# P times V on eight 64x32 array tiles instead of four 128x32 ones

## The chip, the cores and the metric

The kernel runs on one core of a Trainium2 chip. The metric is device time in microseconds of one execution. The core has five engines that matter here, each with an instruction queue of its own that is worked off in order: PE (TensorE, matmuls into PSUM), DVE (VectorE), ACT (ScalarE), POOL (GpSimd, which here works on SBUF only) and SP (SyncE, here the issuer of DMAs). PSUM has eight banks, each 128 partitions by 512 float32.

## The reference

One transformer block with attention and a gated MLP side by side, on x of 2048 tokens by 640:

```python
xn = _layernorm(x)
qkv = (xn @ wqkv)...            # 32 heads, 20 wide
scores = einsum("bhqd,bhkd->bhqk", q, k) * 20 ** -0.5
mask = (i - j >= 0) & (i - j < 256)      # a query sees itself and the 255 keys before it
o = einsum("bhqk,bhkd->bhqd", softmax(where(mask, scores, -1e9)), v)
h = gelu(xn @ w_gate) * (xn @ w_up)
out = x + o @ wo + h @ w_down
```

Everything is float32. The change is in the second `einsum`, the product of the softmax weights P with V.

## The kernel before

The work has three stages. The first (to about 60 us) normalises x, transposes it and begins the projections. The second (about 60 to 571 us) is attention, with the projections and part of the MLP woven between as filling for PE. The third is the rest of the MLP and the output product.

Attention goes in 32 units. Unit u is a group of four heads (g = u // 4) and a chunk of 512 queries (c = u % 4). For a unit the kernel does this:

- `max_pair` (lines 502 to 538): scores once in bfloat16 on 64x64 array tiles, into `ps_m` banks. DVE takes their row maximum (line 526). Eight pairs of banks in a unit.
- `exp_piece` (line 567): the scores again, transposed (keys on the partitions), into a bank `ps_e` (line 581), and ACT writes their exponentials into an SBUF tile `P` (line 583). `pieces(c)` (line 548) packs the key blocks of 128 that a chunk sees into three P tiles called X, Z and Y in `pieces`, of four heads each. For c > 0 there are six key blocks, b-2 to b+3 with b = 4c. X holds b and b-2, Z holds b-1 and b+2, Y holds b+1 and b+3. For c = 0 there are four blocks, 0 to 3. The twelve steps s = 0 to 11 of a unit are X, Z, Y with four heads each.
- `clear` (line 587): after the fourth head of a P tile, POOL zeroes the corners of the band that the mask excludes, one `affine_select` (line 594 or 597) for each 128x128 corner, all four heads at once. Y has three of them, the last for block b+3.
- `av_unit` (line 600): the product. For each key block and each of the four heads one float32 matmul: 128 keys by 32 columns of V (20 of V, one column of ones that gives the softmax sum, the rest unused) as stationary operand, P as the moving one. Head j writes PSUM partitions 32j to 32j+31 of one bank `ps_o`, so four 128x32 tiles of the array work side by side. ACT copies the bank to the SBUF tile `ob` (line 612), and SP stores it (lines 616 and 617).

All of `ps_m`, `ps_e`, `ps_n` and `ps_o` are taken from one pool of six PSUM banks (`bank`, line 497). The first matmul into a bank waits for the engine that read the bank's former content.

What sets the order is written out by hand in `attention` (line 804): a unit has 14 slots. In slot 0 the loop issues two `max_pair`, the product of the unit before, two more `max_pair`, and step s = 0 of its own scores. Steps 1 to 4 are in slot 2, 5 and 6 in slot 4, 7 and 8 in slot 8, and 9 to 11 in slot 10. `defer(n, ...)` puts work n slots later. `clear` of a P tile comes one slot after its last step, so Y is cleared in slot 11, three slots ahead of the product. Each slot ends with some 2.4 dense matmuls of filling. POOL also makes low parts of split weights (line 642, in steps of 128x128), low parts of q and k (line 259) and sums of x (line 739).

A float32 matmul shows as two records of one length in the profile, each with its own weight load. The product therefore has 704 matmuls in the program and 1408 records at line 608: 48 records in a unit with c > 0, 32 in a unit with c = 0.

Of the kernel before, what the change touches and what calls it, by code (L numbers as in the profile page):

```python
# [9 lines left out]
F32 = mybir.dt.float32  # L10
F32R = mybir.dt.float32r
BF = mybir.dt.bfloat16
AF = mybir.ActivationFunctionType
OP = mybir.AluOpType
# [5 lines left out]
C = 512  # L20
# [50 lines left out]
def block_kernel(ctx, tc, x, wqk, wv, wgu, wdo, wdl, out):  # L71
    nc = tc.nc
# [120 lines left out]
    done = set()  # L193
    now = [None]

    def at(slot, fn, *a):
        acts.setdefault(slot, []).append((fn, a))
# [31 lines left out]
    def defer(n, fn, *a):  # L229
        if now[0] is None:  # L230
            fn(*a)
        else:
            at(now[0] + n, fn, *a)
# [190 lines left out]
    with tc.tile_pool(name="lp", bufs=1, side="right") as lp:  # L424
# [5 lines left out]
        ps = psd.tile([128, C], F32, name="ps_u", tag="dn")  # L430
# [48 lines left out]
    vtiles = dict(enumerate(v0[2]))  # L479
    pf.close()  # L480
    psr = pp.enter_context(tc.tile_pool(name="psr", bufs=6, space=PSUM, reuse_waits="tile"))
    ap = pr.enter_context(tc.tile_pool(name="ap", bufs=2, side="right", reuse_waits="tile"))
# [14 lines left out]
    def bank(name):  # L497
        return psr.tile([128, C], F32, name=name, tag="ring")
# [49 lines left out]
    def pieces(c):  # L548
        b = 4 * c
        X = [(b, 0, 0, 384)] + ([(b - 2, 384, 0, 128)] if c else [])  # L550
        Y = [(b + 1, 0, 128, 384), (b + 3, 384, 384, 128)]
        Z = ([(b - 1, 0, 0, 256)] if c else []) + [(b + 2, 256, 256, 256)]
        return X, Z, Y
# [11 lines left out]
    pts = {}  # L565
# [21 lines left out]
    def clear(u, bi):  # L587
        c = u % NC
        pt = pts[u, bi]
        for p in pieces(c)[bi]:  # L590
            for col, diag in diag_tail(*p, c):
# [4 lines left out]
                else:  # L596
                    nc.gpsimd.affine_select(out=a, in_=a, pattern=[[0, 4], [-1, 128]], compare_op=OP.is_ge,  # L597
                                            fill=0.0, base=-1, channel_multiplier=1)

    def av_unit(u):  # L600
        g, c = divmod(u, NC)
        o, v = bank("ps_o"), vtiles[g]
        todo = [(pts[u, bi], *p) for bi, ps in enumerate(pieces(c)) for p in ps]
        for i, (pt, kb, col, q0, n) in enumerate(todo):
            assert (id(v), kb) in done, (u, kb)
            for j in range(4):
                w0_ = kb * 84 + 21 * j
                nc.tensor.matmul(o[32 * j:32 * j + 32, q0:q0 + n], v[:, w0_:w0_ + 32], pt[:, j, col:col + n],  # L608
                                 start=i == 0, stop=i == len(todo) - 1, skip_group_check=True,
                                 tile_position=(0, 32 * j))  # L610
        ob = ap.tile([128, C], F32, name="ob", tag="ob", bufs=1)
        nc.scalar.activation(ob, o, AF.Copy)  # L612

        def store():
            for j in range(4):
                nc.sync.dma_start(od[c].rearrange("(d h) t -> h d t", h=H)[4 * g + j], ob[32 * j:32 * j + DH, :])
            nc.sync.dma_start(sd[c][4 * g:4 * g + 4, :], ob[DH::32, :])

        defer(3, store)

    def load_gu(f):
        raws = []
# [715 lines left out]
    for j, f in enumerate(range(NFA, NF - 1)):  # L1338
        end = f + 1 == NF - 1
        first, second = {i: [] for i in range(4)}, {i: [] for i in range(4)}  # L1340
# [91 lines left out]
    for n, (p, k) in enumerate(steps):  # L1432
        i = n % (NQD + 1)
        if i == 0:
            begun.clear()
            ps = {b: psn.tile([128, C], F32, name=f"ps_{b}", tag=f"b{b}") for b in (1, 2, 5, 3, 6, 4, 7, 8)}
# [71 lines left out]
```

## Time and profile before

| | |
|---|---|
| median of 3 runs | 1047.59 us (1047.58 to 1047.95) |
| the profiled execution, span from first to last instruction | 1046.8 us |
| PE busy | 1035.2 us (99%), 7997 matmul records |
| weight loads (PEld) busy | 827.6 us (79%) |
| DVE busy | 730.8 us (70%) |
| ACT busy | 513.5 us (49%) |
| POOL busy | 333.8 us (32%), in attention 274 of 464 us |
| granted PE clock | 0.999 of full |
| product P times V, line 608 | 84.3 us of PE |
| copies of `ps_o`, line 612 | 19.1 us of ACT, 32 of 597 ns |

The span is what the trace covers. The run times are 0.8 us longer, for what lies ahead of the first and behind the last instruction. Busy time of PE is the union of its records, and a record of a matmul includes its way through the array, so neighbours overlap. Starts of successive rows tell what PE spends, the durations don't. In rows of a timeline the first number is the start, the second the length of the whole merged row, `x48` the number of records in it, and a bracket says how long the engine was idle before and what ended that.

### The profile page before, as it was taken

The numbers are of one execution on the slowest core, as the hardware profiler recorded it, in microseconds if no ns is written. First come the engines' busy times: TensorE is split into PE (matmuls) and PEld (weight loads), VectorE is DVE, ScalarE is ACT, GpSimd is POOL, SyncE is SP. The second block draws the span as 40 slices with busy tenths as digits, with TensorE's granted clock in tenths as the row PEclk, the third lists the DMA queues.
The fourth block names the chain that finished last, engine by engine and source line by source line (L and its number), as shares of the span: only waits on it lengthen the run. The fifth ranks groups of instructions, "written<-read, shape, count | busy, mean of one in ns | idle before, by whom it ended". The sixth has DMA issues, their size and how long they took to land.

```text
span 1046.8 us, 22733 instructions
## 1 busy us (share of the span) xinstructions
PE 1035.2 (99%) x7997; PEld 827.6 (79%) x7997; DVE 730.8 (70%) x2007; ACT 513.5 (49%) x1088; POOL 333.8 (32%) x503
## 2 busy tenths in 40 slices
PE   8999999999999999999999999999999999999998
PEld 7987666666677766666666888888888999999998
DVE  8745656666665556677662677877655889888887
ACT  4444666765665566656565532223324554333332
POOL 5122667766464458474635111110110000000000
PEclk9999999999999999999999999999999999999999
DMA  5651465545332344444322557677217874443342
GB/s 200 189 150 59 135 183 159 179 148 180 96 117 72 111 145 144 139 130 130 112 79 75 191 189 244 213 251 253 100 61 250 270 241 137 134 128 113 125 134 94
DMA packets 105179, 158.56 MB, mean 151 GB/s; under 512 B 15420, under 2 KB 60092, under 8 KB 105064
## 3 DMA queue, kind: packets, MB, share of 16 engines
q1 hardware_dynamic: 102680, 150.95, 45.0%
q10 hardware_dynamic: 2384, 6.16, 1.9%
q8 instruction: 63, 1.03, 0.4%
q14 instruction: 52, 0.43, 0.1%
HBM read 101.78 MB, written 54.92 MB: 150 GB/s over the span
## 4 chain that ended last, share of the span: by engine, by line
PE 92%; DVE 3%; DMA 2%; ACT 1%; POOL 1%; issue 1%; SPq 0%; DVEq 0%; POOLq 0%; ACTq 0%
PE ps_g L952 21%; PE ps L1219 21%; PE ps_d L110 21%; PE ps_e L581 8%; PE ps_o L608 7%; PE ps_v L110 7%; PE ps_m L522 4%; PE ps_g L110 1%; PE ps_t L181 1%; DVE junk L526 1%; DMA qs<-qd 1%; PE ps_d L356 1%; DVE ss L1057 0%; POOL pt L259 0%; DVE at L1057 0%
## 5 line engine op out<-in xcount | busy, mean ns | idle before, releaser
L526 DVE CUSTOM_DVE_ANT_0 junk<-ps_m,mask 128x320 bf16<-128x320 f32 (+2 forms) x512 | 243.2, 475 | 144.5 <-PE ps_m L522 85.5
L583 ACT ACTIVATE P<-ps_e 128x512 f32<-128x512 f32 (+2 forms) x384 | 195.6, 578 | 60.9 <-PE ps_e L581 59.0
L1219 PE MATMUL ps<-wb,at 128*128 128x320 f32 x999 | 156.0, 309 | 0.0
L1219 PEld LDWEIGHTS ps<-wb,at 128*128 128x128 f32 x999 | 148.9, 188 | 0.3
L594 POOL TENSOR_SCALAR_AFFINE_SELECT P<-P 128x512 f32<-128x512 f32 x128 | 83.9, 657 | 141.0 <-ACT P L583 138.3
L581 PE MATMUL ps_e<-qs,ks 124*128 124x128 bf16 (+2 forms) x704 | 108.0, 277 | 0.7 <-DVE mx L526 0.4
L110 PE MATMUL ps_d<-xh,wqh 128*128 128x512 f32 x350 | 104.4, 410 | 0.0
L110 PE MATMUL ps_d<-xl,wqh 128*128 128x512 f32 x350 | 104.2, 409 | 0.0
L110 PE MATMUL ps_d<-xh,wql 128*128 128x512 f32 x350 | 103.8, 409 | 0.0
L1219 PE MATMUL ps<-wt,at 128*128 128x320 f32 x552 | 89.2, 309 | 0.4 <-DVE u L1057 0.4
L581 PEld LDWEIGHTS <-ks 124*128 124x128 bf16 x704 | 50.8, 98 | 47.8 <-issue 30.1
L608 PE MATMUL ps_o<-P,v 128*32 128x384 f32 (+2 forms) x1408 | 84.3, 386 | 0.6 <-DVE mx L526 0.6
L1219 PEld LDWEIGHTS ps<-wt,at 128*128 128x128 f32 x552 | 82.9, 188 | 0.9 <-DVE u L1057 0.9
L597 POOL TENSOR_SCALAR_AFFINE_SELECT P<-P 128x512 f32<-128x512 f32 x112 | 70.8, 643 | 33.7 <-ACT P L583 33.7
L1173 ACT ACTIVATE at<-ss 128x512 fp32r<-128x512 f32 x59 | 37.3, 632 | 89.6 <-DVE ss L1057 89.6
L103 POOL TENSOR_TENSOR wql<-wr,wqh 128x640 fp32r<-128x640 f32 x11 | 17.6, 1607 | 174.0 <-PE ps_g L952 129.4
L110 PEld LDWEIGHTS ps_d<-xh,wql 128*128 128x128 f32 x350 | 63.9, 189 | 11.1 <-issue 0.3
L608 PEld LDWEIGHTS ps_o<-P,v 128*32 128x32 f32 x1408 | 41.5, 110 | 39.0 <-issue 21.1
L110 PEld LDWEIGHTS ps_d<-xl,wqh 128*128 128x128 f32 x350 | 63.8, 189 | 10.5 <-issue 0.2
L110 PEld LDWEIGHTS ps_d<-xh,wqh 128*128 128x128 f32 x350 | 63.4, 189 | 10.7 <-issue 0.3
L259 POOL TENSOR_TENSOR pt<-r,pt 128x512 bf16<-128x512 f32 x40 | 46.8, 1170 | 67.3 <-ACT pt L258 67.2
L612 ACT ACTIVATE ob<-ps_o 128x512 f32<-128x512 f32 x32 | 19.1, 597 | 86.6 <-PE ps_o L608 72.3
(194 smaller groups left out, 1846.0 us busy)
## 6 DMA issues: line engine op xcount, KB each, us to landing
hr<-hd SPq DMA_DIRECT2D x104, 128.0 KB
hd<-he SPq DMA_DIRECT2D x50, 256.0 KB
wr<-wgu SPq DMA_DIRECT2D x27, 320.0 KB
qs<-qd SPq DMA_DIRECT2D x64, 120.0 KB
ks<-kd SPq DMA_DIRECT2D x64, 120.0 KB
xi<-x SPq DMA_DIRECT2D x16, 320.0 KB
qs<-qd SPq DMA_DIRECT2D x64, 80.0 KB
ks<-kd SPq DMA_DIRECT2D x64, 80.0 KB
```

The costliest lines, as they stand in the source:

```text
L110: nc.tensor.matmul(ps, a(k), b(k), start=n == 0, stop=n == 3 * nk - 1)
L259: nc.gpsimd.tensor_tensor(out=pt[:, l, :], in0=r, in1=pt[:, 1, :], op=OP.subtract)
L522: nc.tensor.matmul(ps[64 * h:64 * h + 64, lo:hi], q[rows, j, q0:q0 + 64], keys, start=True, stop=True, tile_position=(64 * r, 64 * h))
L526: nc.vector.tensor_tensor_reduce(out=junk[:, 0:n], in0=ps[:, 0:n], in1=mask[:, 320 - n:320], scale=1.0, scalar=NEG, op0=OP.add, op1=OP.max ...
L581: nc.tensor.matmul(ps[:, col:col + n], k[0:QROWS, j, kc:kc + 128], q[0:QROWS, j, q0:q0 + n], start=True, stop=True)
L583: nc.scalar.activation(pt[:, j, lo:hi], ps[:, lo:hi], AF.Exp, scale=SCALE)
L594: nc.gpsimd.affine_select(out=a, in_=a, pattern=[[0, 4], [1, 128]], compare_op=OP.is_ge, fill=0.0, base=0, channel_multiplier=-1)
L597: nc.gpsimd.affine_select(out=a, in_=a, pattern=[[0, 4], [-1, 128]], compare_op=OP.is_ge, fill=0.0, base=-1, channel_multiplier=1)
L608: nc.tensor.matmul(o[32 * j:32 * j + 32, q0:q0 + n], v[:, w0_:w0_ + 32], pt[:, j, col:col + n], start=i == 0, stop=i == len(todo) - 1, ski ...
L952: nc.tensor.matmul(ps, i, j, start=first and n == 0, stop=n == len(work) - 1, skip_group_check=True)
L1173: nc.scalar.activation(hi[:, 3:7], s, AF.Copy)
L1219: nc.tensor.matmul(ps[bank][:, 0:HD], *work[bank][j], start=bank not in begun, stop=final[p, bank] == n and j == len(work[bank]) - 1, skip ...
```

## The change

The key block of 128 is cut into two halves of 64 keys. Each half is a 64x32 tile of the array (rows 0 to 63 or 64 to 127, columns of head j), so eight tiles work where four did. The halves write two banks. A half of 64 keys is seen by 319 queries at most, so its matmul is up to 320 columns wide where that of the block was up to 384. `windows` gives each half its columns and pairs a lower half with an upper half of the same width (for c = 0 with that of the same block). The six pairs of a unit with c > 0 are 320, 128, 64, 256, 192 and 320 columns wide, 1280 in all where the six blocks had 1536. With c = 0 the four pairs are 320/384, 320/320, 256/192 and 128/64, 1024 and 960 where the blocks had 1152.

ACT copies the first bank to `ob` as before, and the second one into the part of the Y tile of P that belongs to head 0, which the product has read by then. One slot later POOL adds the two, and the store comes one slot later than it did.

```diff
+    def windows(c):
+        r = {}
+        for bi, ps in enumerate(pieces(c)):
+            for kb, col, q0, n in ps:
+                for h in range(2):
+                    first = 128 * (kb - 4 * c) + 64 * h
+                    lo = max(0, first) if kb else 0
+                    hi = min(C, first + 320)
+                    r[h, kb - 4 * c] = bi, kb, col + lo - q0, lo, hi - lo
+        pairs = [((0, 0), (1, 0)), ((0, 3), (1, -2)), ((0, -2), (1, 3)), ((0, 2), (1, -1)), ((0, -1), (1, 2)),
+                 ((0, 1), (1, 1))]
+        if not c:
+            pairs = [((0, d), (1, d)) for d in range(4)]
+        return [[(h, *r[h, d]) for h, d in p] for p in pairs]
+
     def av_unit(u):
         g, c = divmod(u, NC)
-        o, v = bank("ps_o"), vtiles[g]
-        todo = [(pts[u, bi], *p) for bi, ps in enumerate(pieces(c)) for p in ps]
-        for i, (pt, kb, col, q0, n) in enumerate(todo):
-            assert (id(v), kb) in done, (u, kb)
+        halves, v = [bank("ps_o") for _ in range(2)], vtiles[g]
+        todo = windows(c)
+        for i, pair in enumerate(todo):
             for j in range(4):
-                w0_ = kb * 84 + 21 * j
-                nc.tensor.matmul(o[32 * j:32 * j + 32, q0:q0 + n], v[:, w0_:w0_ + 32], pt[:, j, col:col + n],
-                                 start=i == 0, stop=i == len(todo) - 1, skip_group_check=True,
-                                 tile_position=(0, 32 * j))
-        ob = ap.tile([128, C], F32, name="ob", tag="ob", bufs=1)
-        nc.scalar.activation(ob, o, AF.Copy)
+                for h, bi, kb, col, q0, n in pair:
+                    assert (id(v), kb) in done, (u, kb)
+                    rows, w0_ = slice(64 * h, 64 * h + 64), kb * 84 + 21 * j
+                    nc.tensor.matmul(halves[h][32 * j:32 * j + 32, q0:q0 + n], v[rows, w0_:w0_ + 32],
+                                     pts[u, bi][rows, j, col:col + n], start=i == 0, stop=i == len(todo) - 1,
+                                     skip_group_check=True, tile_position=(64 * h, 32 * j))
+        ob, other = ap.tile([128, C], F32, name="ob", tag="ob", bufs=1), pts[u, 2][:, 0, :]
+        nc.scalar.activation(ob, halves[0], AF.Copy)
+        nc.scalar.activation(other, halves[1], AF.Copy)
+        defer(1, lambda: nc.gpsimd.tensor_tensor(out=ob, in0=ob, in1=other, op=OP.add))
...
-        defer(3, store)
+        defer(4, store)
```

Line numbers behind the edit are 18 higher. The order of the instructions moves at three places, shown here for unit 13 (c = 1). A row is a line, an operation, output and inputs and the output's shape; a bracket names the engines or DMA queues that it waits for.

On PE, the product before. It begins with the two blocks of X, goes on with Z, and has Y last. It waits for POOL at each block's first matmul where that block has a cleared corner:

```order
L608 MATMUL ps_o<-P,v 32x384 [waits Activation_49,Pool_49]
L608 MATMUL ps_o<-P,v 32x384 x3
L608 MATMUL ps_o<-P,v 32x128 [waits Pool_49]
L608 MATMUL ps_o<-P,v 32x128 x3
L608 MATMUL ps_o<-P,v 32x256 [waits Pool_49]
L608 MATMUL ps_o<-P,v 32x256 x3
L608 MATMUL ps_o<-P,v 32x256 [waits Pool_49]
L608 MATMUL ps_o<-P,v 32x256 x3
L608 MATMUL ps_o<-P,v 32x384 [waits Pool_49]
L608 MATMUL ps_o<-P,v 32x384 x2
L608 MATMUL ps_o<-P,v 32x384 [waits Activation_49]
L608 MATMUL ps_o<-P,v 32x128 [waits Pool_49]
```

The product now:

```order
L624 MATMUL ps_o<-P,v 32x320 [waits Activation_49,Pool_49]
L624 MATMUL ps_o<-P,v 32x320 [waits Activation_49]
L624 MATMUL ps_o<-P,v 32x320 x6
L624 MATMUL ps_o<-P,v 32x128 [waits Pool_49]
L624 MATMUL ps_o<-P,v 32x128 x7
L624 MATMUL ps_o<-P,v 32x64 x8
L624 MATMUL ps_o<-P,v 32x256 x8
L624 MATMUL ps_o<-P,v 32x192 x8
L624 MATMUL ps_o<-P,v 32x320 x8
```

The second pair is the lower half of block b+3 beside the upper half of b-2. The wait for POOL at its first matmul is for the last corner of Y, which was the last wait of the product before and is now the second one.

On PE, directly behind the product's four `max_pair` banks, the first score of the next unit (s = 0). Before:

```order
L522 LDWEIGHTS qs_166
L522 MATMUL ps_m<-ks_172,qs_166 64x320
L581 LDWEIGHTS ks_170 [waits DMAHW2_49,DMAHW0_49]
L581 MATMUL ps_e<-qs_168,ks_170 128x128 [waits DVE_49]
L581 LDWEIGHTS ks_171
L581 MATMUL ps_e<-qs_168,ks_171 128x384
```

And now:

```order
L522 LDWEIGHTS qs_166
L522 MATMUL ps_m<-ks_172,qs_166 64x320
L581 LDWEIGHTS ks_170 [waits DMAHW2_49,DMAHW0_49]
L581 MATMUL ps_e<-qs_168,ks_170 128x128 [waits Activation_49]
L581 LDWEIGHTS ks_171
L581 MATMUL ps_e<-qs_168,ks_171 128x384
```

With one bank more in use, this score takes the bank of the product's first half. Its wait was for a DVE maximum and is now for ACT's copy of that half (line 628). It is so in the 30 units that have a unit with scores behind them.

On POOL, from the clears of Z to those of the next X. Before:

```order
L597 AFFINE_SELECT P<-P 128x4x128 [waits Activation_49]
L594 AFFINE_SELECT P<-P 128x4x128
L594 AFFINE_SELECT P<-P 128x4x128 [waits Activation_49]
L597 AFFINE_SELECT P<-P 128x4x128
L594 AFFINE_SELECT P<-P 128x4x128
L739 TENSOR_TENSOR tx<-tx,xl_81 128x256 [waits Pool_49] x2
L594 AFFINE_SELECT P<-P 128x4x128 [waits Activation_49]
```

And now:

```order
L597 AFFINE_SELECT P<-P 128x4x128 [waits Activation_49]
L594 AFFINE_SELECT P<-P 128x4x128
L594 AFFINE_SELECT P<-P 128x4x128 [waits Activation_49]
L597 AFFINE_SELECT P<-P 128x4x128
L594 AFFINE_SELECT P<-P 128x4x128
L757 TENSOR_TENSOR tx<-tx,xl_81 128x256 [waits Pool_49] x2
L630 TENSOR_TENSOR ob<-ob,P 128x512 [waits DMAHW3_49,DMAHW4_49,DMAHW2_49,DMAHW5_49,DMAHW1_49,Activation_49]
L594 AFFINE_SELECT P<-P 128x4x128 [waits Activation_49]
```

The addition stands behind what slots 13 and 0 released and ahead of everything of slots 1 and later.

## The prediction

> **What bounds the kernel now.** I read the page first, then the chain of waits, then who waits for whom on PE, and then timelines around the product in single units.
>
> ```profile
> span 1046.8 us, 22733 instructions
> PE 1035.2 (99%) x7997; PEld 827.6 (79%) x7997; DVE 730.8 (70%) x2007; ACT 513.5 (49%) x1088; POOL 333.8 (32%) x503
> PEclk9999999999999999999999999999999999999999
> PE 92%; DVE 3%; DMA 2%; ACT 1%; POOL 1%; issue 1%; SPq 0%; DVEq 0%; POOLq 0%; ACTq 0%
> PE ps_m L522 <- ACT ob L612: 0.7, 2, 0.3
> PE ps_o L608 <- DVE mx L526: 0.6, 1, 0.6
> ```
>
> PE is the bound in every stage, at full clock. Its queue is worked off in order, so whatever PE saves or waits in attention goes into the time one for one. The last two rows are nearly all that PE waited for around the product: 1.3 us in 32 units. The change trades streaming time on PE for new waits, so I follow PE from the start of a product to the first score behind it (line 581), in unit 13 (c = 1):
>
> ```profile
> 300.87 0.47 PE L522 MATMUL ps_m<-ks,qs 60*64 60x64 bf16 x16
> 301.00 0.63 POOL L594 TENSOR_SCALAR_AFFINE_SELECT P<-P 128x512 f32<-128x512 f32 x1
> 301.28 2.80 PE L608 MATMUL ps_o<-P,v 128*32 128x384 f32 x48
> 303.60 0.08 DVE L526 DVE_READ_ACCUMULATOR2_ANT mx<- 128x1 f32 x1
> 304.00 0.47 PE L522 MATMUL ps_m<-ks,qs 60*64 60x320 bf16 x8
> 304.14 0.60 ACT L612 ACTIVATE ob<-ps_o 128x512 f32<-128x512 f32 x1 [2.83 <-PE ps_o L608]
> 304.40 0.39 PE L581 MATMUL ps_e<-qs,ks 124*128 124x128 bf16 x2
> ```
>
> Product start to next matmul 2.72 us, to the score 3.12. The copy starts 0.14 behind that next matmul and ends at 304.74, 0.34 after the score has started. A unit with c = 0:
>
> ```profile
> 286.63 2.15 PE L608 MATMUL ps_o<-P,v 128*32 128x384 f32 x32
> 288.71 0.47 PE L522 MATMUL ps_m<-ks,qs 60*64 60x320 bf16 x8
> 289.11 0.39 PE L581 MATMUL ps_e<-qs,ks 124*128 124x128 bf16 x2
> ```
>
> Here 2.08 and 2.48 us. Each block passes twice (two records). The two units differ by 2 x (1536 - 1152) = 768 columns and 0.64 us: 0.833 ns a column, with four heads side by side. What remains is fixed: 2.72 - 3072 x 0.833 ns = 0.16 us.
>
> **Streaming.** Do both row halves run at once? The scores of line 522 already use 64-row tiles, two row halves by two column halves, into two banks:
>
> ```profile
> L522 PE MATMUL ps_m<-ks,qs 60*64 60x320 bf16 x512 | 30.5, 308 | 0.7 <-ACT ob L612 0.7
> L522 PE MATMUL ps_m<-ks,qs 60*64 60x64 bf16 x288 | 22.3, 200 | 1.4 <-DVE r L273 0.7 <-DMA qs<-qd 0.6
> ```
>
> 308 against 200 ns is 0.42 ns a column, 0.135 us for 320. Eight of these matmuls took 304.00 to 304.40: three rounds at most, where two at a time would need four (0.54). So halves run side by side, and I take eight tiles at the old rate. With c > 0 the product then takes 2 x 1280 x 0.833 ns + 0.16 = 2.29 us; I add 0.03 for starting eight tiles where four start, 2.32. With c = 0: 2 x 1024 x 0.833 + 0.19 = 1.90. By streaming alone 24 x 0.40 + 8 x 0.18 = 11.0 us are saved.
>
> The old product bears on one more point: 48 records, two for each matmul on one tile, fit into 2.72 us only if four tiles run at once although each tile's second pass has to wait for its first. The Trainium skill (TensorE: Matmul & The Clock Gate, Part 3, "The mechanism") has matmuls start and end strictly in program order. With the two passes of a matmul as neighbours in that order, the old product would by this rule take about 4 x 1536 x 0.833 ns = 5.1 us and the new one 8.5; the trace has 2.72, so between columns of heads the rule does not hold here.
>
> **The wait at the score.** The score takes the bank of the first half, so it waits for its copy. PE goes on 0.05 us after a copy ends: in unit 2 it had to wait for one, which ended at 137.95, and went on at 138.00.
>
> ```profile
> 134.49 2.80 PE L608 MATMUL ps_o<-P,v 128*32 128x384 f32 x48
> 136.05 0.64 POOL L594 TENSOR_SCALAR_AFFINE_SELECT P<-P 128x512 f32<-128x512 f32 x1
> 136.74 0.28 PEld L608 LDWEIGHTS ps_o<-P,v 128*32 128x32 f32 x8 [0.37 <-POOL P L594]
> 137.35 0.60 ACT L612 ACTIVATE ob<-ps_o 128x512 f32<-128x512 f32 x1 [2.16 <-DMA qd<-pt]
> 138.00 0.33 PE L522 MATMUL ps_m<-ks,qs 60*64 60x320 bf16 x3 [0.33 <-ACT ob L612]
> 138.26 0.39 PE L581 MATMUL ps_e<-qs,ks 124*128 124x128 bf16 x2
> ```
>
> Product end 2.32 + 0.14 + 0.60 + 0.05 = 3.11 us, where the score could have come at 2.32 + 0.40 = 2.72: a wait of 0.39. Before it was 3.12, so all that the shorter product saves is waited away. Terms, start to score:
> - 20 units with c > 0: 3.11 for 3.12, -0.2 us.
> - Units 2 and 9, which waited for a copy before (138.26 - 134.49 = 3.77, unit 9 the same): 3.11, -1.3 us.
> - 8 units with c = 0: 1.90 + 0.79 = 2.69 for 2.48, +1.7 us.
> - Units 30 and 31, with no score of s = 0 behind: 30 gains 0.40; in 31 a dense matmul takes the bank three matmuls later, and it gains some 0.2. -0.6 us.
>
> Sum -0.4 us.
>
> **The wait for the last corner of Y.** With c > 0 the second pair needs it, 2 x 320 x 0.833 + 0.03 = 0.56 us into the product. Before it was needed by the sixth block, at some 2.4 us. In unit 13 POOL ends it at 301.63, 0.35 after the start: in time. In unit 2 it ends at 136.69, 2.20 after, and even the old order just met it (the weight load of 136.74). Others:
>
> ```profile
> 119.30 0.63 POOL L594 TENSOR_SCALAR_AFFINE_SELECT P<-P 128x512 f32<-128x512 f32 x1
> 119.45 2.80 PE L608 MATMUL ps_o<-P,v 128*32 128x384 f32 x48
> 195.71 2.80 PE L608 MATMUL ps_o<-P,v 128*32 128x384 f32 x48
> 196.44 0.63 POOL L594 TENSOR_SCALAR_AFFINE_SELECT P<-P 128x512 f32<-128x512 f32 x1
> 316.09 0.63 POOL L594 TENSOR_SCALAR_AFFINE_SELECT P<-P 128x512 f32<-128x512 f32 x1
> 316.10 2.80 PE L608 MATMUL ps_o<-P,v 128*32 128x384 f32 x48
> 567.99 2.80 PE L608 MATMUL ps_o<-P,v 128*32 128x384 f32 x48
> 568.60 0.63 POOL L594 TENSOR_SCALAR_AFFINE_SELECT P<-P 128x512 f32<-128x512 f32 x1
> ```
>
> Ends after the start: 0.48 (the first of 24), 1.36, 0.62, 1.24 (the last). Wait = end + 0.05 - 0.56: 0, 0.85, 0.11, 0.73; unit 2 1.69. Read so in all 24, 19 are late, and the waits add up to 9.4 us. With c = 0 the second pair needs the corner before the last, which is late in unit 0 alone (0.4). Together +9.8 us. POOL starts these clears when ACT's last exponential ends, and PE, ACT and POOL keep their distances from slot 8 on, so I expect the same lateness. POOL spans are rough, so I keep 5 us as the lower end.
>
> **The additions.** ACT's second copy (0.60) hides in idle time: 2.83 us before the copy above, and s = 4, which needs the bank of s = 0, comes behind three more scores and two slots of filling. POOL's addition is not in the trace; its nearest rows:
>
> ```profile
> L103 POOL TENSOR_TENSOR wql<-wr,wqh 128x640 fp32r<-128x640 f32 x11 | 17.6, 1607 | 174.0 <-PE ps_g L952 129.4 <-ACT wqh L102 24.5 <-DMA rb<-rd 20.1
> L642 POOL TENSOR_TENSOR wql<-wr,wqh 128x128 fp32r<-128x128 f32 x75 | 34.1, 473 | 1.3 <-ACT wqh L637 1.3
> 105.00:569.00 464.00, 461.25 (x4582) 308.56 (x4578) 289.28 (x1077) 288.94 (x624) 273.66 (x434) 1.00 0.43 131
> L273 DVE TENSOR_TENSOR r<-ps_d,pt 128x512 f32<-128x512 f32 x40 | 27.5, 687 | 31.4 <-ACT pt L277 25.1 <-POOL pt L259 6.1 <-ACT mr L545 0.2
> ```
>
> Between 473 ns for 128 and 1607 for 640, 512 columns are 1.32 us, 42 us in 32 units. POOL has room (273.66 of the 464 us of attention busy, the last but three number of the stretch's row), but the addition waits for the second copy (3.7 us into the product), and behind it stand weight splits, sums of x, q/k low parts (line 259) and the clears. Line 259 frees `r`, for which DVE has already waited 6.1 us (line 273), and behind that stand the maxima that free PE's banks. Cost on PE: 0 if POOL's idle stretches take it all, 7 us if some 12 units lose 0.6 each; I take +2.5, nearer to the idle end. SP's stores wait for the addition, some 2 us longer; behind them stand loads of slot 9, 3 us later: 0. The last two maximum banks wait for the fourth maximum, which ends at 2.40 (303.68) and is needed at 2.32 + 0.16: 0.
>
> **Sum.** -0.4 + 9.8 + 2.5 = +11.9 on 1046.8, 1058.7 us of span. The runs are 0.8 above the profiled span (median 1047.59): 1059.5.
>
> **Rivals.**
> Kept order (chance 12%). In PE the upper half of a head may queue behind the lower half's second pass. Each pass then runs beside one of another width, and the six pairs take 3200 columns a pass for 2560 in all: product 2.86 us, score at 3.65. That adds 0.53 x 22 + 0.4 x 8 = 15: 1074. No row shows how two passes on two row halves queue, since the tiles of line 522 pass once.
>
> Issue (9%). 96 records in 2.16 us are 22 ns each; the densest row is the 16 of 300.87, which take until 301.28, 25.6 ns each. At that pace a unit needs 2.46 us (+7 in all), or +15 if the narrow pairs pay singly: 1067 to 1075. The old product's narrowest blocks needed four records in 128 columns' 0.11 us, 27 ns each, so no row asks for more, and the trace neither shows nor excludes it. The Trainium skill (TensorEngine Tiling (Array Packing), "Instruction Overhead") gives some 60 cycles a matmul; at the 2.4 GHz of its page TensorE: Matmul & The Clock Gate that is 25 ns, an estimate of 2.4 us for a product.
>
> Halves take turns (5%): product 4.4 us, score 2.1 later in 22 units, 1.8 in 8, fewer late corners: about 1115. The rows of line 522 speak against it.
>
> Corners in time (12%; the case that is not slower). If Y's last corner ended by 0.5 us in nearly every unit, as it does in five now, the +9.8 would go, and with the additions hidden the sum is -0.4: 1047.2. It decides at a mean wait of 0.1 us; ACT would have to end its last exponential half a microsecond earlier against PE, and nothing in the change makes it.
>
> **Numbers.** My forecast has 60%: 1059.5. The rest (2%) is left open. The range goes from 1051 (corners at half price, additions free) to 1075 (kept order, issue). A difference under 0.2% (2.1 us) can't be told from none; corners in time lie there or just beyond on the fast side. Faster 0.05, same 0.08, slower 0.87.
>
> **What would show it.** Line 624's row about 2.3 us long where no corner is late; PE waiting at line 581 for `ob` 0.3 to 0.4 us in about 30 units, some 11 us; weight loads of line 624 waiting for POOL's line 594, some 10 us; 64 copies of 0.6 us; an addition of 1.2 to 1.6 us. I am wrong if the product's row stays at 2.7 or more in unit 13 (kept order, issue), or if either wait is missing.

## The result and the profile after

The changed kernel takes 1063.18 us (median of 4 runs, 1062.83 to 1063.57), the kernel before 1047.77 in the runs beside it (1047.58 to 1048.11). The ratio is 1.0144, with a 95% interval of 1.013 to 1.0158: slower, by 15.4 us. The forecast was 1059.5, with a range of 1051 to 1075. In the profiled executions the span went from 1046.8 to 1061.8 us, 15.0 more for a forecast of 11.9. Every run that lists its time and its own span has 1.7 us between the two (here 1063.53 and 1061.8); the 0.8 us that the forecast added came from comparing different executions.

The page of the changed kernel, its busy times and the chain that ended last:

```profile
span 1061.8 us, 25638 instructions
PE 1036.9 (98%) x9405; PEld 838.6 (79%) x9405; DVE 738.3 (70%) x2007; ACT 528.6 (50%) x1120; POOL 374.1 (35%) x535
PE 80%; POOL 5%; DVE 4%; DMA 4%; ACT 3%; issue 2%; SPq 1%; ACTq 0%; DVEq 0%; POOLq 0%
```

PE is as busy as before, but it now stands in 80% of the chain instead of 92%. The shares of POOL, DMA, DVE and ACT have grown: PE waits for other engines at places where it did not wait before. The view of who waits for whom on PE names the two largest new ones (in us, times, longest):

```profile
PE ps_e L581 <- ACT ob L628: 6.1, 22, 0.3
PE ps_o L624 <- POOL P L594: 5.4, 9, 1.5
```

These sums are smaller than the loss, since idle time is counted from the modelled end of the matmul before, and PE still shows the tail of one when it already waits. Starts tell more. Unit 13 (c = 1), the one that the prediction followed, in the changed kernel's timeline:

```profile
306.23 0.63 POOL L594 TENSOR_SCALAR_AFFINE_SELECT P<-P 128x512 f32<-128x512 f32 x1
306.75 2.55 PE L624 MATMUL ps_o<-P,v 64*32 64x320 f32 x96
309.23 0.47 PE L522 MATMUL ps_m<-ks,qs 60*64 60x320 bf16 x8
309.32 0.60 ACT L628 ACTIVATE ob<-ps_o 128x512 f32<-128x512 f32 x1 [2.54 <-PE ps_o L624]
309.97 0.38 PE L581 MATMUL ps_e<-qs,ks 124*128 124x128 bf16 x2 [0.27 <-ACT ob L628]
310.49 1.28 POOL L630 TENSOR_TENSOR ob<-ob,P 128x512 f32<-128x512 f32 x1 [2.12 <-DMA qs<-qd]
```

The last corner of Y ends at 306.86, in time. The product takes 2.48 us to the next matmul (before: 2.73, forecast: 2.32). The score starts 3.22 after the product (before: 3.12, forecast: 3.11), as soon as the first half's copy has ended at 309.92. So the product is 0.24 shorter, and the score comes 0.10 later all the same.

Unit 2, where the last corner is latest:

```profile
134.97 0.77 PE L624 MATMUL ps_o<-P,v 64*32 64x320 f32 x16
136.56 0.63 POOL L594 TENSOR_SCALAR_AFFINE_SELECT P<-P 128x512 f32<-128x512 f32 x1
137.24 2.01 PE L624 MATMUL ps_o<-P,v 64*32 64x128 f32 x80 [1.50 <-POOL P L594]
139.19 0.47 PE L522 MATMUL ps_m<-ks,qs 60*64 60x320 bf16 x8
```

A unit with c = 0 (unit 12):

```profile
291.36 1.95 PE L624 MATMUL ps_o<-P,v 64*32 64x320 f32 x64
293.24 0.91 PE L522 MATMUL ps_m<-ks,qs 60*64 60x320 bf16 x8
293.68 0.08 DVE L526 DVE_READ_ACCUMULATOR2_ANT mx<- 128x1 f32 x1
294.07 0.39 PE L581 MATMUL ps_e<-qs,ks 124*128 124x128 bf16 x2
```

In unit 2 the first pair passes, and the other five stand still until POOL is done at 137.19: 4.21 us in all. In unit 12 the product takes 1.88. The maxima behind it (the row of 293.24) are stretched from 0.47 to 0.91 us: their last bank comes free only when DVE has read a maximum at 293.76. With a product this short, DVE holds PE up as long as the copy would: the copy runs from 293.40 to 294.00, so the score at 294.07, 0.25 us behind its last maximum (0.23 before), hardly waits for it.

Followed from the start of the product to the score (to the 12th matmul behind the product in units 30 and 31) in all 32 units, after against before:

| term | forecast, us | measured, us |
|---|---|---|
| 20 units with c > 0, without their corners | -0.2 | +1.9 |
| units 2 and 9, without their corners | -1.3 | -1.1 |
| 8 units with c = 0, without waits inside the product | +1.7 | +1.8 |
| units 30 and 31, without their corners | -0.6 | -0.25 |
| the last corner, 24 units with c > 0 | +9.4 | +10.0 |
| the corner in unit 0 | +0.4 | +0.4 |
| the second half's bank, units 4 and 20 | 0 | +1.1 |
| additions: unit 24 | +2.5 | +1.3 |
| ahead of unit 0, and between a score and the next product | 0 | -1.2 |
| behind unit 31 | 0 | +1.0 |
| sum | +11.9 | +15.0 |

The waits inside a product are its length less 2.483 us (c > 0) or 1.880 (c = 0), the lengths of undisturbed ones. The -1.2 comes mainly from two waits in the trace of before, 0.65 us for a load of `qs` at 157.71 and 0.69 us for DVE's `r` at 412.29, that the trace after doesn't have; that the change took them away is not shown. The +1.0 lies in the last stage (see the end of the section on the prediction). The second bank and the way of the additions were not foreseen either. Unit 4:

```profile
167.23 2.48 PE L624 MATMUL ps_o<-P,v 64*32 64x320 f32 x64
167.62 0.08 DVE L526 DVE_READ_ACCUMULATOR2_ANT mx<- 128x1 f32 x1
167.76 1.69 PEld L624 LDWEIGHTS ps_o<-P,v 64*32 64x32 f32 x62 [0.40 <-DVE mx L526]
```

In units 4 and 20 the bank of the second half last held a maximum, which DVE is still reading when the product starts: two records go ahead, the other 62 wait 0.53 us. And unit 24, with the way that leads to its wait:

```profile
463.59 1.28 POOL L630 TENSOR_TENSOR ob<-ob,P 128x512 f32<-128x512 f32 x1 [1.16 <-ACT P L629]
464.90 1.40 SPq L634 DMA_DIRECT2D od<-ob  x4
466.88 0.92 SPq L761 DMA_DIRECT2D td<-tx  x2
468.80 0.74 POOL L757 TENSOR_TENSOR tx<-xh 128x256 f32<-128x256 f32 x1 [2.37 <-DMA td<-tx]
475.81 0.63 POOL L597 TENSOR_SCALAR_AFFINE_SELECT P<-P 128x512 f32<-128x512 f32 x1
476.50 1.42 PE L624 MATMUL ps_o<-P,v 64*32 64x320 f32 x48 [0.99 <-POOL P L597]
```

The same wait of POOL in the kernel before, ahead of the product at 466.12:

```profile
458.93 0.74 POOL L739 TENSOR_TENSOR tx<-xh 128x256 f32<-128x256 f32 x1 [3.02 <-DMA td<-tx]
```

The stores of `ob` wait for the addition. Behind them in SP's queue stand the stores of the sums of x (line 761). POOL waits for one of those (line 757 needs the buffer back). It did so before, too, and even longer, but then it went on 7.19 us ahead of the product of unit 24, and now 5.83 us. It is late by that much with everything after it: the corners of unit 24 end up to 2.40 us after the product's start, where before the last ended at 1.02.

### The profile page after: what moved, and what is told of

Its sections match the earlier page's. It is cut to its first block, busy times and chain, and to the rows that moved or that the text cites. A ratio compares the mean times of both kernels' runs of the same rounds, so it can differ in the third digit from the quotient of the medians.

```text
span 1061.8 us, 25638 instructions
## 1 busy us (share of the span) xinstructions
PE 1036.9 (98%) x9405; PEld 838.6 (79%) x9405; DVE 738.3 (70%) x2007; ACT 528.6 (50%) x1120; POOL 374.1 (35%) x535
## 4 chain that ended last, share of the span: by engine, by line
PE 80%; POOL 5%; DVE 4%; DMA 4%; ACT 3%; issue 2%; SPq 1%; ACTq 0%; DVEq 0%; POOLq 0%
PE ps_g L970 21%; PE ps L1237 19%; PE ps_d L110 16%; PE ps_v L110 7%; PE ps_e L581 7%; PE ps_o L624 5%; PE ps_m L522 3%; POOL P L594 2%; DVE junk L526 1%; PE ps_g L110 1%; POOL P L597 1%; ACT ob L628 1%; POOL pt L259 1%; ACT P L583 1%; DMA qs<-qd 1%
## 5 line engine op out<-in xcount | busy, mean ns | idle before, releaser
L624 PE MATMUL ps_o<-P,v 64*32 64x320 f32 (+5 forms) x2816 | 83.1, 351 | 7.2 <-POOL P L594 5.4
L624 PEld LDWEIGHTS ps_o<-P,v 64*32 64x32 f32 x2816 | 50.4, 105 | 27.9 <-POOL P L594 17.4
```

Source lines behind the costliest of these rows:

```text
L624: nc.tensor.matmul(halves[h][32 * j:32 * j + 32, q0:q0 + n], v[rows, w0_:w0_ + 32], pts[u, bi][rows, j, col:col + n], start=i == 0, stop=i ...
```

## The experiments

My theory: the columns saved are there, and four things eat them up and more, of which the wait for the corner (10 us) and the wait for the copy (some 0.34 us in 22 units) are the great ones. The rival to both: PE's waits only show the pace of ACT, POOL or DVE, and a wait that is taken away comes back elsewhere. The runs were made in three groups, in which the kernel before, 1047.77 us beside the changed one, took 1047.98 (the first four in the record: corner last, moved maxima, both, no addition), 1048.32 (fill, corner last with fill, old tiles, whole blocks) and 1048.90 us (the mixed kernels and narrow pairs in the middle). Each ratio is to the kernel before of its own group; differences between runs of two groups are good to about 1 us.

**The corner, with the old tiles.** The kernel before, with its blocks in the new order:

```diff
         todo = [(pts[u, bi], *p) for bi, ps in enumerate(pieces(c)) for p in ps]
+        if c:
+            todo.sort(key=lambda p: (0, 3, -2, 2, -1, 1).index(p[1] - 4 * c))
```

> The kernel before, with its 128x32 tiles, one bank, one copy and no addition; only its blocks stand in the order that needs Y's last corner second (c > 0: +0, +3, -2, +2, -1, +1). The first block passes in 2 x 384 x 0.833 = 0.64 us, so the corner is needed 0.67 into the product. With the ends of the corners in the trace of before (0.43 to 2.20 us after the start) 15 units are late, 7.4 us together. Theory (the order alone makes the corner wait, whatever the tiles): 1055.2. Rival (the corner comes earlier once PE waits for it, or the wait needs the shorter product): within 2 us of the kernel before.

Measured: 1055.04 us, ratio 1.0066 (1.0051 to 1.0081). The profiled span grew by 6.1 us. Of the 24 products 15 are longer by 0.03 us or more, all together by 8.0 us (estimated: 7.4). Up to the score it is 7.3, since unit 2 waits no longer for its copy. Unit 2 (here the product's line is 610):

```profile
134.41 0.85 PE L610 MATMUL ps_o<-P,v 128*32 128x384 f32 x8
135.97 0.64 POOL L594 TENSOR_SCALAR_AFFINE_SELECT P<-P 128x512 f32<-128x512 f32 x1
136.66 2.15 PE L610 MATMUL ps_o<-P,v 128*32 128x128 f32 x40 [1.40 <-POOL P L594]
```

So the order of the blocks alone makes the wait, whatever the tiles, and the ends of the corners in the trace of before price it to within a tenth. In the whole kernel it costs a little less, since the two waits of the trace of before at 157.71 and 412.29 are missing here as well.

**The corner, taken away from the changed kernel.**

```diff
-        pairs = [((0, 0), (1, 0)), ((0, 3), (1, -2)), ((0, -2), (1, 3)), ((0, 2), (1, -1)), ((0, -1), (1, 2)),
-                 ((0, 1), (1, 1))]
+        pairs = [((0, 0), (1, 0)), ((0, 2), (1, -1)), ((0, -1), (1, 2)), ((0, 1), (1, 1)), ((0, 3), (1, -2)),
+                 ((0, -2), (1, 3))]
         if not c:
-            pairs = [((0, d), (1, d)) for d in range(4)]
+            pairs = [((0, d), (1, d)) for d in (0, 2, 1, 3)]
```

> The changed kernel, with the pairs of row halves in another order: the blocks that need Y's last corner come last (c > 0: blocks +0/+0, +2/-1, -1/+2, +1/+1, +3/-2, -2/+3; c = 0: 0, 2, 1, 3). The corner is then needed 1.84 us into the product instead of 0.56. Theory (corner wait): in the changed kernel's trace the late corners stretch 19 products with c > 0 by 10.0 us together, 0.4 in unit 0 and 1.3 in unit 24; of this only unit 2 (0.4) and unit 24 (0.9) stay. 10.4 us less than the changed kernel, 1052.8. The products with c > 0 then take 2.48 us in 23 of 24 units. Rival (POOL, or ACT ahead of it, sets the pace, and what PE saves here it waits at the next exponential or clear): less than 3 us gained, 1060 or more.

Measured: 1053.98 us, ratio 1.0052 (1.0035 to 1.0069), 9.2 less than the changed kernel. The products of 21 of the 24 units with c > 0 are undisturbed. Units 10 and 26 keep 0.34 us: there, too, the second half's bank is late, which the corner had covered. Unit 2 keeps 0.36 us, for the corner itself, as expected. Some waiting did come back elsewhere: in unit 9 the maxima behind the product now wait for DVE, and the score comes 0.60 us later than in other units, in unit 5 0.17. Unit 13 and, from the view of line 624, what its weight loads waited for in all (32 waits and 22.8 us for line 594 in the changed kernel):

```profile
304.11 2.45 PE L624 MATMUL ps_o<-P,v 64*32 64x320 f32 x96
306.48 0.47 PE L522 MATMUL ps_m<-ks,qs 60*64 60x320 bf16 x8
307.26 0.38 PE L581 MATMUL ps_e<-qs,ks 124*128 124x128 bf16 x2 [0.31 <-ACT ob L628]
```

```profile
  POOL P L594: 2.3, 6
```

One thing came as a surprise: the product takes 2.376 us here, 0.107 less than undisturbed ones in the changed kernel, with the same 96 records. I come back to this below. The score still waits for the copy (3.15 after the start, 3.12 before), so that the shorter product again buys nothing.

**The wait at the score, taken away by other banks.** The second pair of maxima behind the product goes to the next slot, and the score takes the bank that the pair would have had:

```diff
                     flush()
-                    pull_max(2, T)
+                    pull_max(1, T)
+                if i == 1 and u:
+                    pull_max(1, T - 1)
```

> The changed kernel, with the second of the two pairs of maxima behind the product moved into the next slot, so that the score of s = 0 takes another bank than that of the product's first half. Theory (score wait): the score comes 1.10 us behind the product's last matmul where 0.76 would do (c > 0, 22 units), and 1.04 where 0.60 would do (c = 0, 8 units): 7.5 + 3.5 = 11 us less than the changed kernel, 1052.2; waits of line 581 for the copy of line 628 gone. Rival (the banks only change places: now the moved pair waits for the second copy, or the score for DVE's maximum): no more than 3 us gained, 1060 or more, and line 522 waits for line 628 or 629 instead.

Measured: 1062.09 us, ratio 1.0133 (1.0117 to 1.0148), only 1.1 less than the changed kernel. The wait for `ob` is gone, and no new wait for `ob` or DVE took its place, so the rival, right in its number (1060 or more), is wrong in its cause. Unit 1:

```profile
122.56 0.39 PE L581 MATMUL ps_e<-qs,ks 124*128 124x128 bf16 x2
122.65 1.00 PE L110 MATMUL ps_d<-xh,wqh 128*128 128x512 f32 x3
123.58 0.33 PE L522 MATMUL ps_m<-ks,qs 60*64 60x320 bf16 x4
123.84 0.73 PE L110 MATMUL ps_d<-xh,wql 128*128 128x512 f32 x2
124.42 1.05 PE L581 MATMUL ps_e<-qs,ks 124*128 124x128 bf16 x8
```

The same unit in the changed kernel:

```profile
123.17 1.00 PE L110 MATMUL ps_d<-xh,wqh 128*128 128x512 f32 x3
124.47 0.83 PE L581 MATMUL ps_e<-qs,ks 124*128 124x128 bf16 x6
```

The score comes 0.48 us earlier after the product's start. But five dense matmuls with the moved pair between them take 124.42 - 122.65 = 1.77 us, where the changed kernel needs 1.30 for the five alone: the pair costs 0.47 in there, and behind another pair it costs 0.15. Breaking into dense matmuls with 64-row tiles costs 0.32 us, what the wait had cost. My edit had a price of its own.

**The same wait, filled instead.** Two of the slot's dense matmuls go ahead of the score:

```diff
+                early = 2.0 if i == 0 and u else 0
+                pull_fill(early)
                 for s in SCORES.get(i, ()) if u < NU else ():
                     exp_piece(u, s)
...
-                pull_fill(RATE / NS)
+                pull_fill(RATE / NS - early)
```

> The changed kernel, with two of the slot's dense matmuls (line 110) ahead of the score of s = 0; nothing moves between bursts and nothing is split. The score then comes some 0.6 us later than it could, and PE has work while the copy of the first half runs. Theory (score wait is real, and the run before lost its gain because the moved pair of maxima broke into the dense matmuls at some 0.45 us): the 0.34 us of 22 units and the 0.44 of 8 go, 11 us, less at most 0.1 a unit where dense matmuls start once more: 1052.2 to 1055.2. Rival (PE doesn't bound the stage there; ACT's or DVE's chain takes up what is saved): 1061 or more, as with the moved pair.

Measured: 1060.54 us, ratio 1.0118 (1.0103 to 1.0133). That is 2.6 us less than the changed kernel (3.4 in the span), between the theory and the rival. Unit 13:

```profile
308.85 0.47 PE L522 MATMUL ps_m<-ks,qs 60*64 60x320 bf16 x8
308.94 0.60 ACT L628 ACTIVATE ob<-ps_o 128x512 f32<-128x512 f32 x1 [2.54 <-PE ps_o L624]
309.24 0.71 PE L110 MATMUL ps_v<-wvh,xh 128*128 128x320 f32 x3
309.79 0.40 PE L581 MATMUL ps_e<-qs,ks 124*128 124x128 bf16 x2
```

PE no longer waits for `ob`. In undisturbed units with c > 0 the score comes some 0.2 us later and the rest of the unit is 0.4 shorter: 0.2 gained of the 0.34. The rest goes where dense matmuls start twice; the first one's distance to the second is 0.25 us there, and 0.145 between others. With c = 0 nothing is gained (units 8 and 28 lose 0.5): there PE waits for DVE at the maxima, as in the row of 293.24 above, and the copy has ended by the time they are through. The fill has no wait to fill, and the second start of dense matmuls remains. Unit 5 loses 0.25, and unit 24 another 0.1.

**Both waits away.** First the order of the blocks with the moved maxima, then with the fill.

> Both edits together: Y's corner last and the moved pair of maxima. If the two waits are separate, their gains add up: 10.4 + 11 = 21.4 us less than the changed kernel, 1041.8, which is 6 less than the kernel before: the streaming that was saved, less the narrow pairs. If they cover one another (POOL's corners come later against PE once the score doesn't hold PE up, or ACT becomes the bound), 1046 or more.

> Y's last corner last, and the two dense matmuls ahead of the score. If the two waits add up: 1054.0 - 11 = 1043, at most 1046 with 0.1 a unit for the new start of dense matmuls; that is 2 to 5 us less than the kernel before. Rival as in the run beside it: 1052 or more.

Measured: 1052.02 us with the moved maxima, ratio 1.0036 (1.0023 to 1.0049), and 1051.45 with the fill, ratio 1.003 (1.0019 to 1.0041). The gains add up: 9.2 + 1.1 would make 1052.9, and 9.2 + 2.6 would make 1051.4. Both estimates had counted the whole wait at the score as a gain, the second less at most 0.1 a unit, and so are 10 and 5 to 8 us too low. The first time lies where its rival put it (1046 or more), but since the gains measured one by one add up, neither result needs one wait to cover the other.

**The addition alone.** The kernel without line 630:

```diff
-        defer(1, lambda: nc.gpsimd.tensor_tensor(out=ob, in0=ob, in1=other, op=OP.add))
```

> The changed kernel without GpSimd's addition (line 630); both copies stay. The output then holds the lower row halves' part of the product alone. By the prediction's term the addition costs PE 2.5 us: 1060.7. By the changed kernel's trace it costs what unit 24 lost, where the stores waited longer for the addition and the corner came 1.3 us later, and nothing else: 1061.9. If POOL's backlog is behind more of the late corners, 4 us or more: 1059 or less.

Measured: 1061.63 us, ratio 1.0127 (1.0112 to 1.0142), 1.5 us less than the changed kernel. The product of unit 24 falls from 3.21 to 1.88 us; no other changes by more than 0.07. Unit 24 in this run:

```profile
474.97 1.95 PE L624 MATMUL ps_o<-P,v 64*32 64x320 f32 x64
475.01 0.63 POOL L594 TENSOR_SCALAR_AFFINE_SELECT P<-P 128x512 f32<-128x512 f32 x1
```

So 41 us of additions cost 1.4 us of span, nearly all of it in one unit; that the way is SP's queue is read from the rows of unit 24 above.

**Narrow pairs.** An undisturbed product of 96 records took 2.483 us in the changed kernel and 2.376 with the narrow pairs (128 and 64 columns) last. In the single records of unit 13, which the timeline merges into one row, the starts of neighbouring tiles are 6.6 ns apart in the first two pairs. In the pair of 64 columns they go to 17 ns, and they stay so in most places until the product ends: the eight tiles are out of step. With the narrow pairs last, the starts are 6.6 ns apart until the last 64 columns. Two runs bear on this. In the first, the four narrow blocks' halves become two whole blocks on 128x32 tiles; in the second, the narrow pairs of the kernel with the corner last stand third and fourth.

```diff
-        return [[(h, *r[h, d]) for h, d in p] for p in pairs]
+        todo = [[(h, 64 * h, 64, *r[h, d]) for h, d in p] for p in pairs]
+        if c:
+            for i, d in ((1, 3), (2, -2)):
+                bi, kb, col, q0, n = r[int(d < 0), d]
+                todo[i] = [(0, 0, 128, bi, kb, col, q0, n)]
...
+        return todo
...
```

> The changed kernel, with blocks +3 and -2 (c > 0) as whole 128x32 tiles into the first half's bank in the place of the two narrow pairs: 32 records fewer a unit, 2 x 64 columns more on each tile. In the changed kernel an undisturbed product with c > 0 takes 2.483 us, where columns and the fixed 0.19 say 2.32; in its trace the starts in the narrow pairs are 13 to 17 ns apart. Theory (pace of records in the narrow pairs): 0.16 - less and 0.107 more streaming, 2.43 us in unit 13 or less; 1 us less in all. Rival (changing between tiles of 64 and 128 rows costs some 0.3 us, as between maxima and dense matmuls): 2.7 us or more, and 5 us more in all. Rival 2 (the 0.16 us lies at the start or end of the product): 2.59, and 2.6 us more in all.

```diff
-        pairs = [((0, 0), (1, 0)), ((0, 2), (1, -1)), ((0, -1), (1, 2)), ((0, 1), (1, 1)), ((0, 3), (1, -2)),
-                 ((0, -2), (1, 3))]
+        pairs = [((0, 0), (1, 0)), ((0, 2), (1, -1)), ((0, 3), (1, -2)), ((0, -2), (1, 3)), ((0, -1), (1, 2)),
+                 ((0, 1), (1, 1))]
```

> The run with Y's corner last, with the two narrow pairs third and fourth of six instead of last. An undisturbed product with c > 0 took 2.483 us with the narrow pairs second and third, 2.376 with them last. If narrow pairs fall behind wherever wide pairs follow (their records come too slowly to keep eight tiles busy): 2.48 here too, and 2.6 us more in all than with the narrow pairs last, besides the corners that are then late (needed 0.99 us into the product: some 2.7 us). If only the start of a product is slow: 2.38.

Measured: 1068.33 us, ratio 1.0198 (1.0181 to 1.0215), with whole blocks, and 1057.45 (2 runs), ratio 1.0078 (1.0058 to 1.0098), with the narrow pairs in the middle. Undisturbed products of the one (line 630) and of the other:

```profile
309.21 2.80 PE L630 MATMUL ps_o<-P,v 64*32 64x320 f32 x80
311.94 0.33 PE L522 MATMUL ps_m<-ks,qs 60*64 60x320 bf16 x4
```

```profile
305.44 2.55 PE L624 MATMUL ps_o<-P,v 64*32 64x320 f32 x96
307.92 0.47 PE L522 MATMUL ps_m<-ks,qs 60*64 60x320 bf16 x8
```

With whole blocks the product takes 2.73 us, 0.25 more than the changed kernel's, of which the columns would make 0.107. But in the records of its unit 13 the starts stay 6.6 ns apart to the end, so the 0.107 us of the narrow pairs (2.483 - 2.376) is not lost here, and whole tiles among half tiles cost all of the 0.25. The starts say where: the first of the whole tiles comes 0.14 us later behind the last half tile than another pair of half tiles would, and the first half tile behind them 0.11 us later than another whole block. The first rival was right, with 5.2 us more than the changed kernel in all. In the middle the narrow pairs cost 0.107 as they did in second place: 2.483. In all the kernel takes 3.5 us more than with them last (3.3 in the span), for the 5.3 expected. The late corners make the products 3.5 us longer (estimated 2.7), but the score comes only 0.07 us later for the narrow pairs, as the wait for the copy takes up the rest; from start to score it is 4.6 us in all, and other waits between the units became shorter. So narrow pairs fall behind wherever wide pairs follow. That only the start of a product is slow is excluded.

**Towards a faster kernel.** The eight units with c = 0 go back to the old product, the others keep Y's corner last; then the fill is added behind the units with c > 0, or else the score is put directly behind the product.

```diff
-        halves, v = [bank("ps_o") for _ in range(2)], vtiles[g]
-        todo = windows(c)
+        halves, v = [bank("ps_o") for _ in range(2 if c else 1)], vtiles[g]
+        if c:
+            todo = windows(c)
+        else:
+            todo = [[(0, bi, *p)] for bi, ps in enumerate(pieces(c)) for p in ps]
+        nr = 64 if c else 128
...
-        defer(4, store)
+        defer(4 if c else 3, store)
```

> Y's corner last (c > 0), and the eight units with c = 0 go back to the kernel before: 128x32 tiles, one bank, one copy, no addition. In the run with the corner last these units still lose 0.25 us each behind the product (units 8, 12, 16, 28), 0.2 in unit 0, 0.7 in units 4 and 20, and 1.2 in unit 24: 3.8 us. Theory (each of these is due to the second bank, the copy or the stores behind the addition): 1054.0 - 3.8 = 1050.2. Rival (unit 24 and units 4 and 20 depend on the neighbours with c > 0, whose stores and banks stay as they are): 1052.5.

> As the run beside it, and two dense matmuls ahead of the score behind the units with c > 0 alone. With the fill each unit with c > 0 keeps 0.21 us against the kernel before, and the units with c = 0 gave 5.3 us away, 4 of them in four units where the maxima behind the short product wait for DVE: 1051.5 - 5.3 = 1046.2, some 2 us less than the kernel before. Rival (as above, the losses of units 4, 20 and 24 stay): 1048.5, no faster than before.

```diff
                     flush()
+                    if u < NU and (u - 1) % NC:
+                        exp_piece(u, 0)
                     pull_max(2, T)
                 for s in SCORES.get(i, ()) if u < NU else ():
-                    exp_piece(u, s)
+                    if s or not u or not (u - 1) % NC:
+                        exp_piece(u, s)
```

> As the first run, but behind the units with c > 0 the score of s = 0 stands directly behind the product, ahead of the four maxima: it then takes a bank whose maximum has been read, and the last maximum takes the first half's bank, some 0.9 us behind the product's last matmul, when its copy has ended or nearly so. If the change of tiles (64 rows, 128, 64 again) costs nothing, 22 x 0.34 = 7.5 us less than the first run: 1042.7. If it costs the 0.25 us that whole tiles among half tiles cost: 1048. If 0.48, as the moved pair did: 1053.

Measured: 1051.22 us, ratio 1.0022 (1.0012 to 1.0031), for the mixed kernel; 1047.93, ratio 0.9987 (0.9977 to 0.9996), with the fill; 1053.42, ratio 1.004 (1.0025 to 1.0055), with the score first. The kernel before took 1048.90 beside them.

The mixed kernel lies between its theory and the rival: units 4 and 20 lose nothing now, but unit 24 keeps 1.15 us: there POOL again waits for the store of line 767 that stands behind the stores of unit 23's sum (2.59 us, until 462.36). In unit 6 the corners have become late (0.66). In its undisturbed units with c > 0 the product is 0.351 us shorter than in the kernel before, and the score comes 0.03 later: this is the change in its purest form, and it gives nothing:

```profile
302.93 2.45 PE L628 MATMUL ps_o<-P,v 64*32 64x320 f32 x96
306.08 0.38 PE L581 MATMUL ps_e<-qs,ks 124*128 124x128 bf16 x2 [0.31 <-ACT ob L632]
```

With the fill, 0.21 a unit comes back, and the kernel is 15 us faster than the changed one; against the kernel before its gain of 0.13% is smaller than the 0.2% that I called a difference, and the profiled spans are 1046.9 and 1046.8. I don't call it faster. With the score first, the first dense matmul in unit 13 starts 3.41 us behind the product's start, for 3.23 in the mixed kernel. The wait has not gone: the last maximum now waits for the copy, and stands 0.29 us (the row of the maxima is 0.78 long instead of 0.47). Without the waits (0.29 here, 0.38 at the score in the mixed kernel) the first dense matmul would come at 3.12 for 2.86, so the changes from 64-row tiles to 128 and to 64 again cost some 0.26 us (an estimate from these starts). The time is the one expected for a price of 0.48, but it is made of a price of 0.26 and a wait that the expectation had put at next to nothing.

```profile
304.62 0.39 PE L581 MATMUL ps_e<-qs,ks 124*128 124x128 bf16 x2
304.74 0.60 ACT L632 ACTIVATE ob<-ps_o 128x512 f32<-128x512 f32 x1 [2.47 <-PE ps_o L628]
304.94 0.78 PE L522 MATMUL ps_m<-ks,qs 60*64 60x320 bf16 x8
305.65 0.70 PE L110 MATMUL ps_v<-wvh,xh 128*128 128x320 f32 x3
```

## Why the prediction was right, and where it was off

- **PE bounds, and the change trades streaming for waits.** Right. The two waits named are the two great ones, in the trace after and in the runs that take them away.
- **Streaming.** The halves run side by side, as read from line 522. With c = 0 the product took 1.88 us (forecast 1.90). With c > 0 it took 2.483 for 2.32. This is the largest term that was sized wrong: 0.107 of the 0.16 is the pair of 64 columns, with wide pairs behind it. The score came 0.10 us later for it in each unit, 2 of the 3.1 us that were missing.
- **The rule that matmuls start and end in order.** I had set it aside. In unit 13 the eight first passes start within 0.05 us, though one matmul of the program makes both passes of a tile, so that in this order each tile's second pass would stand between them. The Trainium skill (TensorE: Matmul & The Clock Gate, Part 3, "The mechanism") has matmuls start and end strictly in program order. By the prediction's estimate that would make the product some 8.5 us long; it took 2.48.
- **The wait at the score.** With c > 0 right in size and kind: 3.22 us from start to score for 3.11; the product was 0.16 longer and the copy started 0.05 sooner behind it. What I didn't see: with c = 0 the fourth maximum, which I priced at nothing for c > 0, is just as late as the copy, since the product is shorter. PE stands at the maxima for it, and the copy costs next to nothing behind that, so for these units the sum (+1.8 for +1.7) was right by luck. Behind unit 30 a score does follow, directly behind the product and without a wait for a copy: the changed wait is in 30 units, as said, but 31 have a score behind them.
- **The corner.** Right: 10.0 us for 9.4 with c > 0, and 0.4 in unit 0. 18 units were late by more than 0.03 us, for 19. POOL did keep its distance to PE.
- **The additions.** +1.3 for +2.5, 1286 ns each for 1.32 us. The way was another: not the sums behind line 259, whose part of DVE's wait at line 273 went from 6.1 to 7.0 us, but SP's queue, which I had put at 0 with the words that loads behind the stores are needed 3 us later. The stores of line 761 stand there too, and POOL waits for them.
- **The second half's bank.** I didn't follow from whom the second bank is taken. In units 4 and 20 it costs 1.1 us, in 10 and 26 another 0.34 each, which the corner hides.
- **The sum.** 3.1 us too low in the span. That it was no more is luck in part: the additions were put 1.2 too high and the two lost waits of before (-1.2) were not in it, against 2.1 for the longer products, 1.1 for the second bank, 1.0 in the last stage and 0.6 for the corner.
- **The rivals.** Kept order and halves in turn are refuted by 2.48 us and the eight starts. Corners in time is refuted. The issue rival took 25.6 ns a record for a limit. Its 2.46 us stood in the place of the 2.16 without the fixed time, so it meant a product of some 2.62 us; it took 2.483, and the same 96 records took 2.376 us in another order, 24.7 ns each even with the fixed time. As one limit for all records it is refuted; that the records of the 64-column pair come too slowly is open (below). The estimate of 2.4 us that the prediction worked out from the Trainium skill (TensorEngine Tiling (Array Packing), "Instruction Overhead": some 60 cycles a matmul) lies between these two lengths.

Still open: why a pair of 64 columns sets the tiles out of step (its 16 records, their weight loads, or both). Being out of step isn't dear by itself: in unit 12 (c = 0) the starts are some 13 ns apart from the second pass on, and the product takes the 1.88 us that its columns ask for. Also open is the last stage of the changed kernel, where PE waits 0.8 us for the output tile `xr` (line 1237), which the trace of before doesn't show. The mixed kernel and the one with the fill show the same wait of 0.8 us, and it takes part of what they gained in attention. It isn't bound to the eight tiles: the changed kernel with the fill and the run with narrow pairs in the middle don't show it.

## What to carry to other kernels

When work on the bounding engine gets shorter, look at who stood behind its old length: a buffer's reader, a late producer, another engine's pace. The corners, copies, maxima and banks here had nearly all fitted under 2.7 us, and each had to be looked up in single units, from one start to the next, with the order of the pieces as the first thing to check.
A wait is worth less than its length if filling it breaks a run of like matmuls: here 0.34 us of waiting gave back 0.2 at best; with the moved pair of maxima the gain was used up by the break, and with the score first the wait only moved.
The additions on an engine with room cost by what stood behind their result in a queue, not by their own time: 1.4 us of span for 41 us of work.

## What the runs showed of the hardware that I had not expected

- With pairs of one width (c > 0) a product's eight tiles run in step, 6.6 ns apart, until a pair of 64 columns; from there starts are 17 ns apart, and the product takes 0.107 us longer if wide pairs follow (2.483 for 2.376).
- A change between tiles of 64 and of 128 rows has a price: 0.32 us for the four matmuls of a pair of maxima among dense matmuls, and 0.25 for two whole blocks among half blocks (0.14 going in, 0.11 coming out). The Trainium skill (TensorEngine Tiling (Array Packing), "Key Properties") says that a change of tiling mode drains TensorE; the price that these runs show agrees with it, though none shows the drain itself.
